# Score steps and weight requests kept away from the joined attention-times-V blocks

## The chip, the cores and the metric

The kernel runs on one core of one Trainium2 chip. The core has a matrix engine (TensorE, PE in the profile, with its weight loads as PEld), three elementwise engines (VectorE = DVE, ScalarE = ACT, GpSimd = POOL), a queue engine (SyncE = SP) that issues most transfers, and 16 DMA engines. The engines run side by side, each through its own instructions in order, and wait for each other on semaphores. The metric is device time in microseconds (us), the median of several executions of one program.

## The reference, cut to what matters

```python
x = A_x                                   # 1 x 2048 x 576, bf16
xn = _layernorm(x)
# A: attention, 32 heads of 18, causal, window of 256 positions
qkv = (xn @ wqkv) ...
scores = einsum("bhqd,bhkd->bhqk", q, k) * (Dh ** -0.5)
mask = (i - j >= 0) & (i - j < 256)
p = softmax(where(mask, scores, -1e9))
a = (einsum("bhqk,bhkd->bhqd", p, v)) @ wo
# B: gated MLP, F = 4608
b = (silu(xn @ w1) * (xn @ w3)) @ w2
return x + a + b
```

Both branches read the same normalised input, and their results are added.

## The kernel before

The 2048 rows are cut into four chunks of 512. Every chunk runs through three stages. First come the projections for q, k and v. Then follows the long stage in which the gate and up products of the MLP are mixed with the attention. The last stage ("phase 2", `p2_list`, L809) multiplies with w2 and wo and adds the input.

The mixed stage is a loop over 36 **units** (`for u in range(NF)`). A unit makes 128 columns of the hidden layer. It is nine **pairs** of matmuls (`unit_pairs`, L738); the two matmuls of a pair use the two halves of the array and run at the same time. After its nine pairs a unit has one tanh on ACT (`unit_tanh`, L747) and two products on DVE (`unit_h`, L753 and L756). A unit takes one of three pairs of PSUM banks (`JOBS`, handed out in turn by `job()`).

Between the pairs the planner puts the attention:

- A **score step** (`score_step`) is four or six short matmuls of q and k into the PSUM banks 6 and 7 (`scores`, L612), one exp on ACT (`exps`, L621) and the masks on POOL (`masks`, L648). A chunk from 1 on has 40 of them. There is only one pair of score banks, so a step's matmuls wait until the exp of the step before has read them. When a step is due is a running sum in units of one pair (`clock`, `nxt`, `soon`).
- An **attention-times-V block** (`pv`, L669) multiplies the probabilities of the steps with V. In chunks 1 to 3 the first block is a *joined* one for two head groups at once (`BLOCKS[c][0] == (0, 1)`). It stands at a fixed place in the middle of a unit (`AT`), takes two pairs of banks, and is drained by four transposes on DVE (`pv_out`, L685), then reciprocals, scalings on POOL (L694) and turns on DVE (L701). A single block `(2,)` follows later at the end of a unit, and a last one in phase 2.
- The finished outputs are sent to `oT` by small transfers on SP's queue (`o_pack`, L726): four for head group 0 and eight smaller ones, two at a time after four successive units, then four for head group 1.

The **weights** w1 and w3 are used in blocks of four units; nine blocks make a chunk. They lie in three buffers `w13`. A buffer is filled by six requests of 192 KB on SP's queue (`load_part`, L322). Six requests become owed (`owed += 6`) after units 3, 7, 11 and so on up to 27, when a block has been used up, for the block after the next two. One owed request is recorded behind pair 3 and one behind pair 8 of a unit (`owe_part`), and waits for that pair's matmul. The first matmul of a block waits for all six requests of its buffer, since all are writers of the key `("w13", sl)`:

```python
r=[("w13", sl)] + (["xnS"] if 4 <= n < 8 else xk(c)), ...
```

Every engine works through its operations in the order in which the Python code records them. SP's queue too is in order: a request behind the small transfers waits until those have been issued.

Phase 2 begins with two short groups of matmuls with wo. The first writes the free pair of banks from `JOBS`, the second the score banks 6 and 7 (`ACC[:] = [[*JOBS[job_ctr % 3], *SC], ...]`), which the exp of the chunk's last score step (number 39, counted from 0) must have read.

Of the kernel before, what the change touches and what calls it, by code (L numbers as in the profile page):

```python
# [164 lines left out]
def bass_parallel_sum__sliding_block__glu_gated_swiglu__prompt_kernel(  # L165
# [21 lines left out]
    NF = F // 128  # L187
# [10 lines left out]
    with ExitStack() as es:  # L198
# [74 lines left out]
        def job():  # L273
            nonlocal job_ctr
            i = job_ctr % 3
            job_ctr += 1
            return JOBS[i]
# [56 lines left out]
        def owe_part(op):  # L334
            nonlocal owed
            if owed:
                owed -= 1
                load_part((op,))
# [338 lines left out]
        def borrow(slots):  # L677

            for i, n in enumerate(slots):
                uqs[2 + i:3 + i] = [pt[:, n, :, :].rearrange("p q r -> p (q r)").bitcast(dt.float32)]  # L680
                uq_keys[2 + i:3 + i] = [[("pt", n)]]

        def pv_out(b, i):
            to = uqs[i]
            add("dve", lambda e: e.transpose(to, PS[:, b, :]), r=[("ps", b)], w=uq_keys[i])  # L685

        def o_recip(i):
            u3 = uqs[i].rearrange("p (n d) -> p n d", d=32)
            add("dve", lambda e: e.reciprocal(rden[i][:], u3[:, :, Dh]), r=uq_keys[i], w=[("rden", i)])

        def o_scale(i):
            u3 = uqs[i].rearrange("p (n d) -> p n d", d=32)
            o3 = oq[:, :].rearrange("p (n d) -> p n d", d=32)[:, :, 0:Dh]
            add("pool", lambda e: e.tensor_tensor(  # L694
                o3, u3[:, :, 0:Dh], rden[i][:].unsqueeze(2).to_broadcast([128, CH // 32, Dh]), ALU.mult),
                r=uq_keys[i] + [("rden", i), "oq0"], w=["oq"])
# [307 lines left out]
        BLOCKS = [((0,), (1,), (2,))] + [((0, 1), (2,))] * 3  # L1004
        PV_AFTER = (20, 18, 18, 18)
        START = (60, 46, 46, 46)
        AT = ((NF, 0), (18, 3), (18, 5), (18, 7))
        main, rest = span_main, span_last
        late_spans = {0: [(main, 2, 5, 0, 1, "act")], 1: [(main, 2, 5, 1, 2, "act"), (main, 2, 5, 2, 5, "sp")],
                      **{u: [(rest, 2, 5, u - 2, u - 1, "act")] for u in (2, 3, 4)},  # L1010
# [3 lines left out]
        for c in range(NC):  # L1014
            NS = len(steps_of(c))
            att = [(g, s) for g in range(G) for s in range(NS)]
# [13 lines left out]
            nxt = soon = start  # L1030
            clock = 0.0
            done = 0
            pv_ready = {}
            free = [("pt", n) for n in range(NPT)]
            free += [("sh", n) for n in range(4)]
            early = [("h", n) for n in range(4 if c == 0 else 0, NHP)]
            side = {}
            jobs = {}
            next_pv = 0
            turned = {}  # L1040

            def later(u, what):
                side.setdefault(u, []).append(what)
# [25 lines left out]
            def pv_block(u, mid=False):  # L1069
                nonlocal next_pv, clock, free, job_ctr, nxt, soon  # L1070
                block = BLOCKS[c][next_pv]
                assert u > turned.get(c, -1) + 1, (c, u, turned)
                next_pv += 1
                pairs = [job() for _ in block]
                for j, banks in zip(block, pairs):
                    pv(c, j, banks)
                clock += PV_COST * len(block)
                if len(block) == 2:
                    nxt, soon = max(nxt, clock + 14), max(soon, clock + 14)
                groups = range(2 * block[0], 2 * block[-1] + 2)  # L1080
                was = [pt_of[(c, g, s)] for g in groups for s in range(NS)]
                assert all(NF - 2 * NHP + 2 * n > u for kind, n in was if kind == "h"), (c, u)
                was = [sl for sl in was if sl[0] != "h"]
                lent = [n for kind, n in was if kind == "pt"][-2:] if len(block) == 2 else []
                free += [sl for sl in was if sl not in [("pt", n) for n in lent]] + [("pt", n) for n in lent]

                def drain(pairs=pairs, lent=lent):
                    borrow(lent)
                    for i in range(2 * len(pairs)):
                        pv_out(pairs[i // 2][i % 2], i)  # L1090
                    for i in range(2 * len(pairs)):
                        o_recip(i)
                    o_scale(0)

                drain() if mid else later(u, drain)
                job_ctr += mid
                k = 0
                for i, g in enumerate(groups):
                    for half in range(2):
                        k += 1 if (i, half) not in ((0, 1), (2, 1)) else 0  # L1100
                        later(u + k, lambda g=g, half=half: o_turn(g, half))
                    if i + 1 < len(groups):
                        later(u + k, lambda i=i: o_scale(i + 1))
                turned[c] = u + k
                for i, j in enumerate(block):
                    later(u + (4 + 3 * i if c else 5), lambda j=j: o_pack(j, "sp"))
                    for n in range(4, 12, 2 if c else 1) if j == 0 else ():
                        later(u + n // 2 + 3 if c else u + n + 1,
                              lambda n=n: o_pack(0, "sp", n, n + 2) if c else o_pack(0, "act", n, n + 1))
# [19 lines left out]
            for u in range(NF):  # L1129
                at_u = u  # L1130
                if c == 0 and u == 0:
                    owed += 6
                if u in loads:
                    for i in loads[u]:
                        xslot[(c + 1) * TB + i] = load_x((c + 1) * TB + i)
                b0 = jobs[u] = job()
                for n in range(9):
                    into = nxt - (clock + 9 - n)
                    if done < len(att) and (done < len(early) or free) and (clock >= nxt or (n == 8 and into < 3 and clock >= soon)):
                        spaced_step()  # L1140
                    if next_pv == 0 and AT[c] == (u, n):
                        pv_block(u, True)
                    op = unit_pairs(c, u, n, n + 1, b0[0])
                    clock += 1
                    if n in (3, 8):
                        owe_part(op)
                unit_tanh(u, b0[0])
                if u % 4 == 3 and u < NF - 8 and (c or u != 15):
                    owed += 6
                if next_pv in pv_ready and clock >= pv_ready[next_pv] and (next_pv or not AT[c][1]):  # L1150
                    pv_block(u)
                unit_h(u, b0[0])
                for what in side.pop(u, []):
                    what()
                if u in stat:
                    t = (c + 1) * TB + stat[u]
                    for part in range(3):
                        ln_stats(t, xslot[t], part)
                if u in xt:
                    xn_send((c + 1) * TB + xt[u])  # L1160
                if u in apply:
                    t = (c + 1) * TB + apply[u]
                    ln_apply(t, xslot[t])
                for span, a, b, n0, n1, eng in late_spans.get(u, []) if c == 0 else []:
                    span(a, b, only=slice(n0, n1), **({"q_eng": eng} if span is main else {"eng": eng}))
                if c == 0 and u == 8:
                    add("dve", lambda e: e.memset(oT[:, 4, :].bitcast(dt.float32), 0.0), w=["oTz"])
                if c == 0 and u == 13:
                    for t in range(4):
                        r0 = 4 * Dh + 252 * (t // 2)  # L1170
                        rows = A_wo[r0:r0 + 252, :].rearrange("(s p d) f -> p s d f", p=2, d=Dh)[t % 2, :, :, :]
                        add("sp", lambda e, t=t, rows=rows: e.dma_start(wo[0:126, t, :], rows),
                            dma="wo", **{"j" if t else "w": ["wo"]})
                if c == 0 and u == 18:
                    rows = A_wo[0:4 * Dh, :].rearrange("(n d) f -> n d f", d=Dh)
                    add("sp", lambda e: e.dma_start(wo[126:128, 0:4, :], rows[:, 0:2, :].rearrange("n d f -> d n f")),
                        j=["wo"], dma="wo")
                    for p in range(2):
                        add("sp", lambda e, p=p: e.dma_start(wo[64 * p:64 * p + 64, 4, :], rows[:, 2:Dh, :]),
                            j=["wo"], dma="wo")  # L1180
                if c == 0 and u in (20, 22, 24, 26):
                    load_w2(0, (u - 20) // 2, "act" if u < 24 else "sp")
                if u == 31:
                    xs = [load_x(c * TB + tt) for tt in range(TB)]
# [9 lines left out]
            n = -3  # L1194
# [62 lines left out]
```

## Time and profile before

| | |
|---|---|
| median of 3 runs | 558.32 us (557.24 to 558.74) |
| profiled execution, its own time | 558.11 us |
| its span, first to last instruction | 556.4 us |
| granted TensorE clock | 1.00 |
| PE busy | 551.5 us, 99% of the span |
| DVE, ACT, POOL busy | 313.0, 260.3, 160.6 us |
| HBM read | 71.29 MB |

The profile's own time is longer than its span by 1.7 us, which lie outside the instructions. In the views, a row of the timeline or of the chain of waits has the start in us from the span's start, then the duration, the engine, the line of the kernel, and the number of instructions merged into it; a square bracket tells how long the engine sat idle before it, and what ended that. PE's matmuls overlap, so that a row's duration is longer than the time until the next one starts.

### The profile page before, as it was taken

The numbers are of one execution on the slowest core, as the hardware profiler recorded it, in microseconds if no ns is written. First come the engines' busy times: TensorE is split into PE (matmuls) and PEld (weight loads), VectorE is DVE, ScalarE is ACT, GpSimd is POOL, SyncE is SP. The second block draws the span as 40 slices with busy tenths as digits, with TensorE's granted clock in tenths as the row PEclk, the third lists the DMA queues.
The fourth block names the chain that finished last, engine by engine and source line by source line (L and its number), as shares of the span: only waits on it lengthen the run. The fifth ranks groups of instructions, "written<-read, shape, count | busy, mean of one in ns | idle before, by whom it ended". The sixth has DMA issues, their size and how long they took to land.

```text
span 556.4 us, 18249 instructions
## 1 busy us (share of the span) xinstructions
PE 551.5 (99%) x8022; PEld 365.3 (66%) x8022; DVE 313.0 (56%) x587; ACT 260.3 (47%) x365; POOL 160.6 (29%) x380
## 2 busy tenths in 40 slices
PE   8999999999999999999999999999999999999998
PEld 4555445677688855577776665557777667555776
DVE  7466798520468887741056887773105566868211
ACT  7456776100387757600047775760005677676000
POOL 4323454300035435430003533452000333343000
PEclk9999999999999999999999999999999999999999
DMA  9998898567567953656846895365684685332660
GB/s 252 214 202 179 191 207 204 143 179 185 140 142 170 163 144 102 165 138 186 196 106 138 171 187 132 89 165 155 156 202 91 138 176 153 105 103 67 162 164 23
DMA packets 128038, 86.00 MB, mean 155 GB/s; under 512 B 35702, under 2 KB 125646, under 8 KB 127958
## 3 DMA queue, kind: packets, MB, share of 16 engines
q1 hardware_dynamic: 89138, 62.80, 50.1%
q10 hardware_dynamic: 38820, 22.02, 15.6%
q8 instruction: 63, 1.03, 0.8%
q14 instruction: 17, 0.14, 0.1%
HBM read 71.29 MB, written 2.36 MB: 132 GB/s over the span
## 4 chain that ended last, share of the span: by engine, by line
PE 98%; DMA 1%; ACT 0%; DVE 0%; issue 0%
PE ps L738 51%; PE ps L809 29%; PE ps L492 10%; PE ps L612 6%; PE ps L669 3%; DMA xp<-in_A_x_dram 1%; DVE stats L388 0%; ACT hT L382 0%; PE ps L421 0%; ACT sd L361 0%; DVE ofin L831 0%; ACT xnT L434 0%; DVE mv L391 0%
## 5 line engine op out<-in xcount | busy, mean ns | idle before, releaser
L738 PE MATMUL ps<-xnT,w 64*128 64x512 bf16 x1400 | 187.9, 376 | 0.0
L738 PE MATMUL ps<-xnS,w 64*128 64x512 bf16 x1120 | 157.4, 376 | 0.0
L809 PE MATMUL ps<-w,hT 64*128 64x288 bf16 x2292 | 143.9, 282 | 0.0
L753 DVE SCALAR_TENSOR_TENSOR gs<-th,ps 128x512 bf16<-128x512 bf16 x144 | 98.1, 681 | 76.6 <-ACT th L747 75.8
L809 PEld LDWEIGHTS ps<-w,hT 64*128 64x128 bf16 x2292 | 111.8, 94 | 29.6 <-issue 0.2
L738 PEld LDWEIGHTS ps<-xnT,w 64*128 64x128 bf16 x1400 | 83.3, 94 | 51.9 <-issue 0.7
L621 ACT ACTIVATE pt<-ps 128x1024 bf16<-128x1024 f32 (+1 forms) x92 | 93.2, 1013 | 42.0 <-PE ps L612 41.7
L747 ACT ACTIVATE th<-ps 128x512 bf16<-128x512 f32 x144 | 85.6, 595 | 34.3 <-PE ps L738 33.7
L756 DVE SCALAR_TENSOR_TENSOR hT<-gs,ps 128x512 bf16<-128x512 bf16 x144 | 98.9, 687 | 4.9
L738 PEld LDWEIGHTS ps<-xnS,w 64*128 64x128 bf16 x1120 | 65.6, 94 | 41.9
L648 POOL TENSOR_TENSOR pt<-pt,mk 128x128 int32<-128x128 int32 (+1 forms) x164 | 67.4, 435 | 51.8 <-ACT pt L621 51.7
L505 ACT ACTIVATE stage<-ps 128x512 bf16<-128x512 f32 x16 | 9.6, 598 | 142.8 <-PE ps L492 140.5
L648 POOL TENSOR_TENSOR hT<-hT,mk 128x128 int32<-128x128 int32 (+1 forms) x52 | 20.8, 421 | 165.0 <-ACT hT L621 165.0
L840 DVE TENSOR_TENSOR ofin<-ps,xp 128x288 bf16<-128x288 f32 x31 | 12.2, 451 | 89.0 <-PE ps L809 89.0
L612 PE MATMUL ps<-qv,kv 64*128 64x320 bf16 (+4 forms) x528 | 55.8, 260 | 0.0
L612 PEld LDWEIGHTS ps<-qv,kv 64*128 64x128 bf16 x528 | 31.4, 94 | 21.6 <-ACT pt L621 0.5
L621 ACT ACTIVATE stage<-ps 128x1024 bf16<-128x1024 f32 (+1 forms) x32 | 32.4, 1011 | 15.6 <-PE ps L612 14.1
L492 PE MATMUL ps<-xnT,wp 64*128 64x512 bf16 (+1 forms) x360 | 39.1, 355 | 0.0
L621 ACT ACTIVATE hT<-ps 128x1024 bf16<-128x1024 f32 (+1 forms) x28 | 28.5, 1016 | 10.0 <-PE ps L612 9.9
L648 POOL TENSOR_TENSOR stage<-stage,mk 128x128 int32<-128x128 int32 (+1 forms) x56 | 22.0, 413 | 26.8 <-ACT stage L621 26.7
L492 PEld LDWEIGHTS ps<-xnT,wp 64*128 64x128 bf16 x360 | 20.6, 94 | 12.5 <-ACT va L541 0.4
L701 DVE STREAM_TRANSPOSE od<-oq 128x256 bf16<-128x256 bf16 x64 | 25.8, 427 | 3.1 <-POOL oq L694 3.1
(76 smaller groups left out, 344.2 us busy)
## 6 DMA issues: line engine op xcount, KB each, us to landing
w<-in_B_w_dram SPq DMA_DIRECT2D x210, 192.0 KB, 4.1
w<-in_B_w_dram ACTq DMA_DIRECT2D x70, 288.0 KB, 3.5
xp<-in_A_x_dram SPq DMA_DIRECT2D x29, 144.0 KB, 3.4
out_dram<-ofin SPq DMA_DIRECT2D x31, 72.0 KB, 3.1
xnS<-xnT SPq DMA_DIRECT2D x8, 256.0 KB, 5.2
oT<-od SPq DMA_DIRECT2D x56, 36.0 KB
pt<-in_A_wqkv_dram SPq DMA_DIRECT2D x4, 288.0 KB, 5.4
hT<-in_B_w_dram SPq DMA_DIRECT2D x6, 192.0 KB, 6.2
```

Of the source, the lines that this page charges most:

```text
L492: op = add("pe", lambda e, out_=out_, st=st, mv=mv, n=n, r0=r0, first=first: e.matmul(out_, st, mv, start=first, stop=(part == 1 and n == ...
L612: add("pe", lambda e, r0=r0, out_=out_, kb=kb, q0=q0, nb=nb: e.matmul(out_, kb4[r0:r0 + 64, g, kb + NV - NB, :] if kb < 0 else kv[r0:r0 + ...
L621: add("act", lambda e: e.activation(pt_slot(sl)[:, 0:w, :], PS[:, SC[0]:SC[1] + 1, 0:w].rearrange("p r q -> p q r"), ACT.Exp, scale=scale) ...
L648: add("pool", lambda e, vb=vb, mm=mm: e.tensor_tensor(vb, vb, mm, ALU.mult), r=(key if n == 0 else []) + ["mk"], **{"w" if n == 0 else "j" ...
L669: add("pe", lambda e, p=p, q=q, pr=pr, sl=sl, g=g, pos=pos, q0=q0, nb=nb, col=col, first=first, n=n: e.matmul(PS[32 * q:32 * q + VW, banks ...
L701: add("dve", lambda e: e.transpose(od[i][:, g % 2, c0:c0 + CH // 2], oq[:, c0:c0 + CH // 2]), r=["oq", "oq0"], **{"j" if half or g % 2 els ...
L738: op = add("pe", lambda e, n=n, r0=r0, r=r, k=k, src=src: e.matmul(PS[:, b0 + r, :], wt[r0:r0 + 64, k, fl * 128:(fl + 1) * 128], src, star ...
L747: add("act", lambda e: e.activation(th[i][:], PS[:, bg, :], ACT.Tanh, scale=0.5), r=[("ps", bg)], w=[("th", i)])
L753: add("dve", lambda e: e.scalar_tensor_tensor(out=gs[i][:], in0=th[i][:], scalar=1.0, in1=PS[:, bg, :], op0=ALU.add, op1=ALU.mult), r=[("t ...
L756: add("dve", lambda e: e.scalar_tensor_tensor(out=hT[:, u, :], in0=gs[i][:], scalar=0.5, in1=PS[:, bu, :], op0=ALU.mult, op1=ALU.mult), r= ...
L809: op = add("pe", lambda e: e.matmul(PS[:, bank, 0:w], stat, move, start=new, stop=False, skip_group_check=True, **tile), r=keys, after=hel ...
L840: add("dve", lambda e: e.tensor_tensor(ofin[:, o, :], PS[:, bank, 0:HD], xp[xs[n]][:, d0:d0 + HD], ALU.add), r=[("ps", bank), ("xp", xs[n] ...
```

## The change

```diff
-        AT = ((NF, 0), (18, 3), (18, 5), (18, 7))
+        HOLD = 15
+        AT = ((NF, 0), (18, 8), (19, 1), (19, 3))
...
                 if len(block) == 2:
-                    nxt, soon = max(nxt, clock + 14), max(soon, clock + 14)
+                    nxt, soon = max(nxt, clock + 17), max(soon, clock + 17)
...
                     into = nxt - (clock + 9 - n)
-                    if done < len(att) and (done < len(early) or free) and (clock >= nxt or (n == 8 and into < 3 and clock >= soon)):
+                    ahead = 9 * (AT[c][0] - u) + AT[c][1] - n
+                    still = next_pv == 0 and 0 <= ahead < HOLD
+                    if not still and done < len(att) and (done < len(early) or free) and (clock >= nxt or (n == 8 and into < 3 and clock >= soon)):
                         spaced_step()
...
-                    if n in (3, 8):
+                    if n in (3, 8) and not (c and 16 <= u < 20):
                         owe_part(op)
```

Four things change in chunks 1 to 3; chunk 0 stays as it was.

1. The joined block comes five pairs later: chunk 1 from unit 18 pair 3 to unit 18 pair 8, chunk 2 from (18, 5) to (19, 1), chunk 3 from (18, 7) to (19, 3).
2. In the 15 pairs ahead of it no score step is put, and behind it the next one comes 17 instead of 14 counts later.
3. No weight request is recorded in units 16 to 19.
4. What follows from these by the planner: the steps that were held come later and closer, and the requests move.

The requests of the mixed stage, by the unit whose pairs 3 and 8 they stand behind (the same in chunks 1 to 3, save that chunk 3 has no last row):

| weight block | first used in unit | before, units | after, units |
|---|---|---|---|
| 6 | 24 | 16 to 18 | 20 to 22 |
| 7 | 28 | 20 to 22 | 23 to 25 |
| 8 | 32 | 24 to 26 | 26 to 28 |
| 0 of the next chunk | its first | 28 to 30 | 29 to 31 |

The small transfers to `oT` after the joined block stand in SP's queue after units 22 to 26 before, and in chunk 1 still do. In chunks 2 and 3 they stand one unit later now. In order, of chunk 1 after the change: four behind unit 22, two behind 23, two behind 24, six behind 25 (two of head group 0, four of group 1), two behind 26. In chunks 2 and 3: four behind unit 23, two behind 24, two behind 25, six behind 26, two behind 27.

The score steps in the changed program:

| | chunk 1 | chunk 2 | chunk 3 |
|---|---|---|---|
| none between | (16, 3) and (20, 7) | (17, 3) and (21, 0) | (16, 8) and (21, 2) |
| spacing behind it, pairs | 7 | 7 | 7 |
| steps between pair 8 of unit 22 and unit 24 | 2 | 1 | 1 |
| from the first pair of unit 24 to that of unit 28 | 5 | 6 | 5 |
| from the first pair of unit 28 to that of unit 32 | 5 | 5 | 6 |
| single block ahead of unit (before: 30 in all) | 32 | 31 | 32 |
| step 39 ahead of pair (before: unit 34 pair 7) | (35, 8) | (34, 8) | (35, 8) |

Before, the steps behind the joined block are mostly 8 pairs apart and at the end 9, and the joined block of chunk 1 has a step right ahead of it. The number of matmuls, exps, masks and transfers is the same in both programs.

## The prediction

> **What bounds the kernel now.** I read the page first: busy times, then the chain of work that ended last, then the transfers.
>
> ```profile
> span 556.4 us, 18249 instructions
> PE 551.5 (99%) x8022; PEld 365.3 (66%) x8022; DVE 313.0 (56%) x587; ACT 260.3 (47%) x365; POOL 160.6 (29%) x380
> PE 98%; DMA 1%; ACT 0%; DVE 0%; issue 0%
> ```
>
> PE sets the end nearly everywhere, so any wait that PE gets is paid in full, and a gain can come only out of time in which PE stands. The sums over the three mixed stages (chunks 1, 2, 3) show how much of that there is: stretch, length, then busy time of each engine, clock, DMA share, GB/s.
>
> ```profile
> 155.42:237.83 82.41, 82.41 (x1125) 57.08 (x1122) 63.15 (x116) 58.71 (x76) 36.27 (x87) 1.00 0.68 149
> 292.57:375.58 83.01, 82.45 (x1124) 50.04 (x1122) 62.88 (x116) 58.81 (x76) 36.23 (x87) 1.00 0.71 148
> 430.32:512.65 82.33, 82.33 (x1125) 49.49 (x1122) 56.89 (x96) 57.94 (x76) 32.34 (x76) 1.00 0.51 123
> ```
>
> PE is busy without a break in chunks 1 and 3, and stands for 83.01 - 82.45 = 0.56 us in chunk 2. The chain of waits has it (start, length, what), the timeline says where it falls, and the sums around it what the DMA engines did:
>
> ```profile
> 333.00 2.50 PE ps L669 x157
> 338.84 0.56 issue
> ```
>
> ```profile
> 339.40 0.19 PE L612 MATMUL ps<-qv,kb 64*128 64x64 bf16 x1 [0.56 <-issue]
> 333.00:336.00 3.00, 3.00 (x198) 2.50 (x200) 2.39 (x5) 0.63 (x1) 0.75 (x2) 1.00 1.14 213
> 338.40:339.60 1.20, 0.64 (x12) 0.32 (x8) 0.73 (x2) 0.60 (x1) 0.00 (x0) 1.00 0.30 99
> ```
>
> The wait is in a score step 3.4 us behind the joined block (333.00 to 335.49); nothing that the profile shows released it ("issue"). In the block PE works through 198 matmuls and 200 weight loads in 3 us while the DMA engines are full (share 1.14); I take it for instructions that came late. It is the only thing this change could win.
>
> **The price list.** From the chain of waits (start, length, what):
>
> ```profile
> 361.21 1.30 PE ps L669 x93
> 364.56 0.22 PE ps L612 x4
> 364.78 1.94 PE ps L738 x18
> ```
>
> A unit of nine pairs is 1.94 us (a pair 0.216), a score step 0.22, a single block 1.30. Now one unit of chunk 1 in the timeline of PE, and SP's queue from the same place on:
>
> ```profile
> 207.72 1.24 PE L738 MATMUL ps<-xnT,w 64*128 64x512 bf16 x10
> 208.80 0.38 PE L612 MATMUL ps<-qv,kv 64*128 64x320 bf16 x4
> 209.02 1.03 PE L738 MATMUL ps<-xnS,w 64*128 64x512 bf16 x8
> 209.88 1.03 PE L738 MATMUL ps<-xnT,w 64*128 64x512 bf16 x8
> ```
>
> ```profile
> 208.14 0.60 SPq L322 DMA_DIRECT2D w<-in_B_w_dram  x1
> 208.78 4.75 SPq L726 DMA_DIRECT2D oT<-od  x6
> 213.57 1.32 SPq L322 DMA_DIRECT2D w<-in_B_w_dram  x2
> 214.93 1.30 SPq L726 DMA_DIRECT2D oT<-od  x2
> 216.28 1.32 SPq L322 DMA_DIRECT2D w<-in_B_w_dram  x2
> 217.64 4.45 SPq L726 DMA_DIRECT2D oT<-od  x6
> 222.13 1.42 SPq L322 DMA_DIRECT2D w<-in_B_w_dram  x2
> ```
>
> The ten matmuls at 207.72 are pair 8 of unit 22 and the first four pairs of unit 23. The request behind pair 8 goes out at 208.14, 0.42 us after that pair starts. Unit 24 starts one pair after 209.88, at 210.10. On SP's queue six small transfers hold up what follows by 4.79 us (208.78 to 213.57) or 4.49 (217.64 to 222.13), two of them by 1.35, two requests by 1.36, one by 0.64 (208.14 to 208.78). Time from request to landing, min/median/max over the 23 requests from 185 to 226 us, and of the one at 208.14 alone:
>
> ```profile
> DMA to landing us min/median/max: 3.1/3.6/4.1
> w<-in_B_w_dram SPq DMA_DIRECT2D x1, 192.0 KB, 3.5
> ```
>
> I take 3.5 us, the row with the very surroundings of the critical request, and keep 3.1 and 4.1 as ends.
>
> **Part 1, block 6 in unit 24.** Before, its last request stands behind unit 18, five units ahead of its use. Now it stands behind pair 8 of unit 22. Count from the start of that pair: request at 0.42, landed at 0.42 + 3.5 = 3.92. PE reaches unit 24 after one pair, unit 23 and its score steps: 0.22 + 1.94 + 0.22 = 2.38 in chunks 2 and 3 (the trace itself has 210.10 - 207.72 = 2.38 for that), 2.60 with the two steps of chunk 1. PE waits 1.32, 1.54 and 1.54 us, **4.4 us** together. With landings of 3.1 or 4.1 it is 3.2 or 6.2. Even the quickest landing misses the unit, so this term cannot vanish. Nothing can cover it: the wait is in PE's own queue ahead of all later pairs and steps.
>
> [...]
>
> **Part 2, blocks 7 and 8 behind the small transfers.** Their requests now come close behind block 6's, in a queue that before already lagged (requests behind unit 24 went out at 213.57, when SP had worked off the six small transfers). I run the queue on from the same zero.
>
> Chunk 1: SP free at 1.06; four small transfers (4/6 of 4.79, an estimate: 3.19) to 4.25; two requests to 5.61; two small to 6.96; two requests to 8.32; two small to 9.67; the last two requests of block 7 go out at 9.67 and 10.35, landed 13.85. PE has started unit 24 at 3.92 and needs 4 x 1.94 and five steps, 3.92 + 7.77 + 1.10 = 12.79: it waits **1.06** for unit 28. Then six small to 15.52, two requests to 16.88, two small to 18.23, two requests to 19.59, the last at 20.27, landed 23.77. PE: 13.85 + 7.77 + 1.10 + 1.30 for the single block = 24.02: no wait.
>
> Chunks 2 and 3: the first two requests of block 7 go out ahead of the small ones, the second when pair 8 of unit 23 has started (2.58), SP free at 3.24; four small to 6.43; then in turns of 1.36 and 1.35 to 9.14; last request 9.82, landed 13.32. PE reaches unit 28 at 13.01 (six steps) and 12.79 (five): waits **0.31 and 0.53**. On: 10.50, two small 11.85, two requests 13.21, six small 17.70, two requests 19.06, two small 20.41, last request 21.09, landed 24.59. PE reaches unit 32 at 13.32 + 7.77 + 1.30 + 1.10 = 23.49 and with six steps 23.71: waits **1.10 and 0.88**.
>
> Part 2 is 3.9 us. Bounds: 0 if SP works off its queue 1.1 us quicker per chunk, and some 3 us more if a request's issue drags in each chunk, as it does at times (1522 ns at most instead of a median of 614, in chunk 2):
>
> ```profile
> L322 SPq DMA_DIRECT2D w<-in_B_w_dram x18: 595/614/1522, 340.3 to 367.3; - x18
> ```
>
> **Part 3, the start of phase 2.** Step 39 moves from unit 34 to one pair ahead of the end in chunks 1 and 3. Its exp must have left banks 6 and 7 before the second short group of phase 2. In chunk 1 before (step at 235.07, exp to 236.53, phase 2 at 237.67) there is room:
>
> ```profile
> 235.07 0.27 PE L612 MATMUL ps<-qv,kb 64*128 64x256 bf16 x2
> 235.50 1.03 ACT L621 ACTIVATE pt<-ps 128x1024 bf16<-128x1024 f32 x1 [0.43 <-PE ps L612]
> 237.67 0.41 PE L809 MATMUL ps<-wo,oT 64*128 64x288 bf16 x4
> ```
>
> The exp ends 1.46 us after the step begins. Now PE gets there after the step (0.22), a pair (0.22) and the first group (half of the 0.24 from 237.67 to the next at 237.91, 0.12): 0.56. It waits 0.9 us in each of the two chunks, **1.8 us**; ACT could add to it, and only another order of PE's could take it away.
>
> ```profile
> 237.91 1.27 PE L809 MATMUL ps<-w,hT 64*128 64x288 bf16 x18
> ```
>
> **Part 4, at little or nothing.** The number of steps and blocks stays, so PE's own work does. Steps 7 pairs apart are 7 x 0.216 + 0.22 = 1.73 us apart, and the exp is gone after 1.46: 0.27 to spare. A step ahead of a unit's first pair (five in all) finds ACT in the tanh of the unit before and may lose some 0.1 us; most of it falls into the waits above, which shrink by as much. In chunk 1 the joined block ends one pair before unit 19, which writes the block's first banks. DVE needs 713 + 668 ns for them from the block's middle on:
>
> ```profile
> L685 DVE STREAM_TRANSPOSE uq<-ps 128x512 f32<-128x512 f32 x13 | 9.3, 713 | 26.6 <-PE ps L669 26.4
> L685 DVE STREAM_TRANSPOSE ofin<-ps 128x512 f32<-128x512 f32 x13 | 8.7, 668 | 0.0
> ```
>
> 1.38 against 1.30 + 0.22 = 1.52 us on PE: hidden, 0 to 0.3 us if DVE starts late. The gain is the 0.56 us of chunk 2, between 0 (the wait moves to where the requests now bunch) and 0.56.
>
> **The sum.** 4.4 + 3.9 + 1.8 - 0.6 = 9.5 us on the profile's own 558.11 gives 567.6. That execution is 0.2 us under the median of 558.32, which I leave aside: forecast **567.5 us**, 1.6% slower. Low end: landings of 3.1 and a quick SP queue, 3.2 + 0 + 0 - 0.6, 560.7, unlikely all together; high end 6.2 + 3.9 + 3 + 1.8 - 0, 573.
>
> **The rivals.**
>
> - *Only the first deadline is missed.* SP catches up or the queue's lag costs less than I count, so part 2 is gone: 4.4 + 1.8 - 0.6, 563.7 us. For it: the waits of part 2 are small differences of long sums. Against: each wait of PE moves later requests back too.
> - *The other side: instructions come in time and the weights too.* The mechanism is the change's own: without requests and steps around the joined block, PE's instructions arrive, and the 0.56 us of chunk 2 goes. It decides if a request lands within 2.38 - 0.42 = 1.96 us. Then the time is 557.5 to 558, no difference that can be told. Against it stands the minimum of 3.1. A gain over 0.3% would need 1.7 us of PE standing still, and the stages have 0.56.
> - *PE's clock drops in the waits.* If each of my ten waits (two, three and three in parts 1 and 2, two in part 3) were followed by some 3 us at half speed, it would cost 1.5 us apiece, 15 more: 582. Against: the clock stays 1.00 across the 0.56 us wait in the sums above, though no wait of 1.5 us is in these stages. [...]
> - *The queue drags.* Slow issues in each chunk make parts 1 and 2 some 5 us larger: 572 to 573.
>
> **How the numbers follow.** Forecast 0.74, first deadline only 0.12, the other side 0.05, clock 0.02, dragging queue 0.07. The range 562 to 572 us holds the forecast with its bounds and the first rival, and leaves about 0.15 outside. A difference below 0.3% (1.7 us) cannot be told from none. Slower by more than that: all cases but the second rival, 0.94; within: 0.04; faster: 0.02, for what I may have missed.
>
> **What would show it.** Right: PE idle ahead of L738, ended by a DMA of w, about 1.3 to 1.5 us once in each of chunks 1 to 3 (unit 24), and shorter ones four and eight units on; an idle of 0.9 us ahead of L809 ended by ACT's exp at the start of phase 2 in chunks 1 and 3; PE's busy time in the mixed stages unchanged; no "issue" wait near 339. Wrong: no such waits, landings under 2 us, or waits of PE on ACT or DVE in the middle of the units.

## The result, and the profile after

| | before | after |
|---|---|---|
| median of 6 runs | 557.78 us (557.21 to 558.74) | 575.32 us (573.90 to 579.01) |
| ratio, 95% interval | | 1.032 [1.029, 1.035] |
| profiled execution, its own time | 558.11 us | 576.36 us |
| its span | 556.4 us | 574.6 us |

The change makes the kernel 17.5 us slower; the forecast was 9.5. The direction and the kinds of waits are as predicted, the size is not. The profiled execution lies 1.0 us above the median, and its span grew by 18.2 us; the accounts below are of that execution.

The page of the changed kernel: the span, the busy times, the chain of work that ended last, and the group of matmuls that opens a unit (behind the bar its busy time, the mean in ns, the idle time ahead of it and what ended that).

```profile
span 574.6 us, 18249 instructions
PE 555.7 (97%) x8022; PEld 374.2 (65%) x8022; DVE 312.5 (54%) x587; ACT 260.4 (45%) x365; POOL 160.7 (28%) x380
PE 92%; DMA 4%; issue 2%; ACT 1%; DVE 1%; SPq 0%
L738 PE MATMUL ps<-xnT,w 64*128 64x512 bf16 x1400 | 192.8, 377 | 12.7 <-DMA w<-in_B_w_dram 7.7
```

Before, the same group had no idle time ahead of it:

```profile
L738 PE MATMUL ps<-xnT,w 64*128 64x512 bf16 x1400 | 187.9, 376 | 0.0
```

The number of instructions is the same. PE was the chain to 98%; now it is 92%, 4% of it is DMA, and the group that opens the units has 12.7 us of idle time ahead of it. The sums over the three mixed stages say where: first before, cut at the same instructions as after (first matmul of the first unit to first matmul of phase 2), then after.

```profile
155.14:237.67 82.53, 82.53 (x1127) 57.20 (x1122) 63.25 (x116) 58.99 (x76) 36.11 (x86) 1.00 0.68 149
292.36:375.42 83.06, 82.50 (x1125) 50.05 (x1121) 62.90 (x116) 59.02 (x76) 36.07 (x86) 1.00 0.71 148
430.12:512.49 82.37, 82.37 (x1124) 49.49 (x1121) 56.90 (x96) 58.14 (x76) 32.34 (x76) 1.00 0.51 123
```

```profile
154.99:242.58 87.59, 83.00 (x1125) 62.69 (x1121) 63.28 (x117) 58.02 (x75) 34.73 (x83) 1.00 0.65 139
298.25:387.91 89.66, 84.78 (x1125) 51.54 (x1122) 62.88 (x116) 59.19 (x76) 35.88 (x86) 0.98 0.64 136
442.62:529.76 87.14, 83.11 (x1124) 50.46 (x1121) 57.37 (x97) 57.19 (x75) 31.65 (x75) 1.00 0.46 116
```

The stages grew by 5.06, 6.60 and 4.77 us, 16.4 together. PE stands for 87.59 - 83.00 = 4.59, 4.88 and 4.03 us. Its busy time grew as well, by 0.47, 2.28 and 0.74 us, though it does the same work. Some 0.2 us of that, an estimate, go with each wait: a matmul's row (377 ns in the mean) is longer than the 216 ns until the next pair starts, and at a wait this overlap is lost. What is left over in chunk 2, about 1.5 us, goes with a clock of 0.98. The rest of the 18.2 us is at the start of phase 2 in chunks 1 and 3, about 1 us each. The view of waits (engine, tile, line, releaser: us in total, times, longest) gives PE's two largest:

```profile
PE ps L738 <- DMA w<-in_B_w_dram: 7.7, 5, 2.4
PE ps L738 <- issue: 5.0, 4, 2.1
```

The timeline of PE places them, and the four smaller ones in the joined blocks (L669) and at the start of phase 2 (L809):

```profile
210.52 1.04 PE L738 MATMUL ps<-xnT,w 64*128 64x512 bf16 x8 [0.92 <-issue]
221.98 1.04 PE L738 MATMUL ps<-xnT,w 64*128 64x512 bf16 x8 [2.38 <-DMA w<-in_B_w_dram]
233.72 1.04 PE L738 MATMUL ps<-xnT,w 64*128 64x512 bf16 x8 [1.29 <-DMA w<-in_B_w_dram]
243.66 0.30 PE L809 MATMUL ps<-wo,oT 64*128 64x288 bf16 x2 [0.78 <-ACT pt L621]
341.66 0.56 PE L669 MATMUL ps<-pt,va 64*20 64x320 bf16 x24 [0.57 <-DVE hT L756]
354.53 0.39 PE L738 MATMUL ps<-xnT,w 64*128 64x512 bf16 x2 [0.97 <-issue]
365.06 1.04 PE L738 MATMUL ps<-xnT,w 64*128 64x512 bf16 x8 [1.27 <-DMA w<-in_B_w_dram]
377.58 0.90 PE L738 MATMUL ps<-xnT,w 64*128 64x512 bf16 x4 [2.06 <-issue]
485.91 1.00 PE L669 MATMUL ps<-pt,va 64*20 64x320 bf16 x60 [0.27 <-DVE hT L756]
498.41 0.82 PE L738 MATMUL ps<-xnT,w 64*128 64x512 bf16 x6 [1.03 <-issue]
508.51 0.61 PE L738 MATMUL ps<-xnT,w 64*128 64x512 bf16 x4 [1.06 <-DMA w<-in_B_w_dram]
520.90 1.04 PE L738 MATMUL ps<-xnT,w 64*128 64x512 bf16 x8 [1.68 <-DMA w<-in_B_w_dram]
530.85 0.29 PE L809 MATMUL ps<-wo,oT 64*128 64x288 bf16 x2 [0.78 <-ACT pt L621]
```

In each chunk the three waits ahead of L738 are those for units 24, 28 and 32. Four of the nine are put down to "issue", but they are waits for weights too, as the transfers show. For the first of them, here is the last request of block 6 in chunk 1, and its time to landing:

```profile
207.24 0.59 SPq L322 DMA_DIRECT2D w<-in_B_w_dram  x1
```

```profile
w<-in_B_w_dram SPq DMA_DIRECT2D x1, 192.0 KB, 3.2
```

207.24 + 3.2 = 210.44, and PE goes on at 210.52. The clock after the longest wait of chunk 2 (stretch, length, busy times, then the clock as the third number from the end):

```profile
376.00:377.50 1.50, 0.00 (x0) 0.00 (x0) 0.80 (x2) 0.64 (x2) 1.02 (x3) 1.00 1.08 228
377.50:381.30 3.80, 3.72 (x22) 1.86 (x24) 1.26 (x3) 1.02 (x1) 0.67 (x1) 0.55 1.14 227
```

For about 3.4 us (0.45 of 3.8 us missing, at half speed) PE ran at half clock; from 378.50 to 380.50 the clock is 0.50. Of the six executions three have a mean clock of 1.000 (573.90 to 575.30 us), so that stretch is not in every one.

SP's queue in chunk 1, from behind the request above to block 8:

```profile
207.88 3.40 SPq L726 DMA_DIRECT2D oT<-od  x4
211.33 1.40 SPq L322 DMA_DIRECT2D w<-in_B_w_dram  x2
212.77 1.34 SPq L726 DMA_DIRECT2D oT<-od  x2
214.16 2.18 SPq L322 DMA_DIRECT2D w<-in_B_w_dram  x2
216.38 1.30 SPq L726 DMA_DIRECT2D oT<-od  x2
217.72 1.33 SPq L322 DMA_DIRECT2D w<-in_B_w_dram  x2
219.09 4.44 SPq L726 DMA_DIRECT2D oT<-od  x6
...
226.42 7.42 SPq L322 DMA_DIRECT2D w<-in_B_w_dram  x10
```

Block 7's requests stand in turn with the small transfers, as predicted. The last two go out from 217.72 on. The prediction's chain had them at 9.67; with its zero at 206.82, so that its request at 0.42 is the one at 207.24, that is 206.82 + 9.67 = 216.49.

### The profile page after: what moved, and what is told of

It reads as the page before. It is cut to its first block, busy times and chain, and to the rows that moved or that the text cites. A ratio compares the mean times of both kernels' runs of the same rounds, so it can differ in the third digit from the quotient of the medians.

```text
span 574.6 us, 18249 instructions
## 1 busy us (share of the span) xinstructions
PE 555.7 (97%) x8022; PEld 374.2 (65%) x8022; DVE 312.5 (54%) x587; ACT 260.4 (45%) x365; POOL 160.7 (28%) x380
## 4 chain that ended last, share of the span: by engine, by line
PE 92%; DMA 4%; issue 2%; ACT 1%; DVE 1%; SPq 0%
PE ps L738 47%; PE ps L809 28%; PE ps L492 9%; PE ps L612 5%; DMA w<-in_B_w_dram 4%; PE ps L669 2%; DMA xp<-in_A_x_dram 0%; ACT pt L621 0%; DVE hT L756 0%; DVE gs L753 0%; ACT th L747 0%; DVE stats L388 0%; ACT hT L382 0%; PE ps L421 0%; ACT sd L361 0%
## 5 line engine op out<-in xcount | busy, mean ns | idle before, releaser
L738 PE MATMUL ps<-xnT,w 64*128 64x512 bf16 x1400 | 192.8, 377 | 12.7 <-DMA w<-in_B_w_dram 7.7
L738 PE MATMUL ps<-xnS,w 64*128 64x512 bf16 x1120 | 159.8, 378 | 0.0
L809 PE MATMUL ps<-w,hT 64*128 64x288 bf16 x2292 | 143.9, 282 | 0.0
L809 PEld LDWEIGHTS ps<-w,hT 64*128 64x128 bf16 x2292 | 112.9, 94 | 28.6 <-issue 0.4
L738 PEld LDWEIGHTS ps<-xnT,w 64*128 64x128 bf16 x1400 | 87.2, 94 | 63.6 <-DMA w<-in_B_w_dram 11.9
L738 PEld LDWEIGHTS ps<-xnS,w 64*128 64x128 bf16 x1120 | 69.5, 94 | 37.8 <-issue 0.5
L492 PE MATMUL ps<-xnT,wp 64*128 64x512 bf16 (+1 forms) x360 | 39.0, 355 | 0.0
L492 PEld LDWEIGHTS ps<-xnT,wp 64*128 64x128 bf16 x360 | 20.5, 94 | 12.6 <-ACT va L541 0.4
L694 POOL TENSOR_TENSOR oq<-uq,rden 128x288 bf16<-128x288 f32 x13 | 8.8, 674 | 67.3 <-DVE rden L689 67.3
```

What stands on the lines that cost most here:

```text
L492: op = add("pe", lambda e, out_=out_, st=st, mv=mv, n=n, r0=r0, first=first: e.matmul(out_, st, mv, start=first, stop=(part == 1 and n == ...
L738: op = add("pe", lambda e, n=n, r0=r0, r=r, k=k, src=src: e.matmul(PS[:, b0 + r, :], wt[r0:r0 + 64, k, fl * 128:(fl + 1) * 128], src, star ...
L809: op = add("pe", lambda e: e.matmul(PS[:, bank, 0:w], stat, move, start=new, stop=False, skip_group_check=True, **tile), r=keys, after=hel ...
```

## The experiments

Times are medians, each ratio is against the kernel before on the same chip.

**The request rule alone.** Once it is taken out of the changed kernel, once put alone into the kernel before.

```diff
-                    if n in (3, 8) and not (c and 16 <= u < 20):
+                    if n in (3, 8):
```

> The changed kernel with the old rule for requests (behind pairs 3 and 8 of every unit); joined block, hold and spacing as changed. Theory (late requests cost nearly all, some 13.5 us of PE's waits in units 24, 28 and 32 and 1.7 us of half clock behind one of them): 560 to 561 us, no wait of PE for w in the mixed stages; what is left is about 1 us at the start of phase 2 in chunks 1 and 3 and about 1 us in the joined blocks of chunks 2 and 3. Rival (the denser score steps or the later block cost as much themselves): over 565 us.

Measured: 561.14 us, ratio 1.006 [1.005, 1.008]. No wait for weights is left in any chunk; the waits at phase 2 and in the joined block stay. The mixed stage of chunk 2 in the sums:

```profile
293.88:377.78 83.90, 83.06 (x1125) 49.59 (x1122) 62.76 (x116) 58.98 (x76) 35.70 (x86) 1.00 0.71 146
```

It is back within 0.8 us of before; those of chunks 1 and 3 (82.94 and 82.88 us) within 0.4 and 0.5. So the request rule costs 575.3 - 561.1 = 14.2 us.

```diff
-                    if n in (3, 8):
+                    if n in (3, 8) and not (c and 16 <= u < 20):
```

> The kernel before with the new rule for requests alone (none in units 16 to 19). Theory: 570 to 573 us, with waits of PE for w at units 24, 28 and 32 of chunks 1 to 3 of the changed kernel's size, none at the start of phase 2 or in the joined blocks. Rival (the requests are late only together with the moved block and steps): under 563 us.

Measured: 571.86 us, ratio 1.025 [1.024, 1.027], 14.0 us: the two ways of taking the rule agree in the total, though not in its parts. In detail the expectation missed. Units 24 and 28 wait in all three chunks, but unit 32 only in chunk 3, for 0.7 us (0.52 us of idle time and the lost overlap); what makes the time up is two stretches at half clock, behind the waits of unit 28 in chunks 1 and 2. In chunk 2 the clock is 0.79 over 8 us (364.00 to 372.00), 1.7 us missing. The stretch in chunk 1, first in the timeline of PE, then in the sums:

```profile
222.14 1.53 PE L738 MATMUL ps<-xnT,w 64*128 64x512 bf16 x8 [2.00 <-DMA w<-in_B_w_dram]
```

```profile
223.00:226.40 3.40, 3.40 (x24) 1.70 (x22) 0.00 (x0) 1.23 (x2) 0.31 (x1) 0.56 0.37 100
```

**The small transfers out of the requests' way.** In the changed kernel the transfers of the joined block go out three units later in chunks 1 to 3.

```diff
-                    later(u + (4 + 3 * i if c else 5), lambda j=j: o_pack(j, "sp"))
+                    later(u + (4 + 3 * i + 3 * (len(block) == 2) if c else 5), lambda j=j: o_pack(j, "sp"))
...
-                        later(u + n // 2 + 3 if c else u + n + 1,
+                        later(u + n // 2 + 3 + 3 * (len(block) == 2) if c else u + n + 1,
```

> The changed kernel with the small transfers to oT of the joined block three units later, so that the requests of weight block 7 stand ahead of them in SP's queue. Theory (units 28 and 32 are late because of SP's queue behind the small transfers): the waits at unit 24 stay at 1.1 us or so each, those at 28 and 32 (some 10 us of the sum) shrink to under 3 us, the half clock goes: 564 to 567 us. Rival (it is the time from request to landing, or the chain of one late block on the next, whatever stands between in the queue): 572 us or more.

Measured: 570.01 us, ratio 1.020 [1.018, 1.023], between the ranges of theory and rival. The four executions scatter (567.62 to 572.61 us), and the profiled one is the longest: it also has a wait of 2.5 us for the DMA of `wv` (L492), which is loaded once at the start, far ahead of the mixed stages that the edit touches, and its mean clock is 0.994. Chunks 1 and 3 did as the theory said: only unit 24 waits, and their stages shrank to 83.78 and 84.19 us. Chunk 2 has a cost of the experiment's own. The single block comes a unit earlier there, its turns on DVE wait until the late transfers have read `od` (the longest such wait of the run is 5.2 us), and the products of the last units queue behind them on DVE:

```profile
383.53 1.69 PE L738 MATMUL ps<-xnT,w 64*128 64x512 bf16 x8 [3.20 <-DVE hT L756]
```

Behind it the clock is 0.60 over 4.00 us (383.00 to 387.00), 1.6 us missing. So chunk 2 was run again with two units instead of three.

```diff
-                    later(u + (4 + 3 * i if c else 5), lambda j=j: o_pack(j, "sp"))
+                    later(u + (4 + 3 * i + (2 if c == 2 else 3) * (len(block) == 2) if c else 5), lambda j=j: o_pack(j, "sp"))
...
-                        later(u + n // 2 + 3 if c else u + n + 1,
+                        later(u + n // 2 + 3 + (2 if c == 2 else 3) * (len(block) == 2) if c else u + n + 1,
```

> As the run with the small transfers three units later, but in chunk 2 only two units later, so that they are over before the single block's turns on DVE need their buffer. Theory (SP's queue behind the small transfers made the waits at units 28 and 32): waits for w at unit 24 alone, about 1.2 us in each of chunks 1 to 3, no half clock in the mixed stages; 564 to 566 us, which is the run with the old rule for requests plus 3.6 us. Rival (lateness passes from block to block even with a free queue): 568 us or more in undisturbed runs, with waits for w at unit 28 or 32.

Measured: 566.34 us, ratio 1.015 [1.013, 1.017]. Units 28 and 32 wait in no chunk, and the clock is 1.00. The sums of chunks 1 and 3, and what is left of the side effect in chunk 2 (DVE's turn, then PE):

```profile
155.00:238.72 83.72, 82.70 (x1127) 61.71 (x1121) 63.17 (x117) 58.04 (x76) 34.62 (x83) 1.00 0.65 140
434.94:519.00 84.06, 82.80 (x1124) 50.46 (x1121) 57.41 (x97) 57.19 (x76) 31.56 (x75) 1.00 0.48 120
```

```profile
376.16 0.77 DVE L701 STREAM_TRANSPOSE od<-oq 128x256 bf16<-128x256 bf16 x2 [3.20 <-DMA oT<-od]
...
378.29 1.04 PE L738 MATMUL ps<-xnT,w 64*128 64x512 bf16 x8 [1.19 <-DVE hT L756]
```

The small transfers standing in front of blocks 7 and 8 are worth at least 575.3 - 566.3 = 9.0 us of the 14, the half clock included; the side effect, a wait of 1.2 us, hides some of it.

**Catching up.** The changed kernel keeps its pause in units 16 to 19, and records four requests a unit instead of two in units 20 to 22.

```diff
-                    if n in (3, 8) and not (c and 16 <= u < 20):
+                    if (n in (3, 8) or c and 20 <= u < 23 and n in (1, 5)) and not (c and 16 <= u < 20):
```

> The changed kernel with four requests instead of two in each of units 20 to 22 (behind pairs 1, 3, 5 and 8), so that block 6 is requested by (21, 3) and block 7 by (22, 8), as before; still none in units 16 to 19. Theory: no wait for w, the time of the run with the old rule for requests within 1 us, 560 to 561 us. Rival (requests bunched in three units land so late, or take instructions and the small transfers along, that PE waits elsewhere): over 563 us.

Measured: 561.12 us, ratio 1.006 [1.005, 1.008], the same as without the pause. Only unit 24 of chunks 2 and 3 still waits a little:

```profile
349.43 0.39 PE L738 MATMUL ps<-xnT,w 64*128 64x512 bf16 x2 [0.57 <-issue]
```

So the pause itself is not the cost; it is that the requests stay late behind it.

**A shorter pause.** The changed kernel with three units without requests instead of four.

```diff
-                    if n in (3, 8) and not (c and 16 <= u < 20):
+                    if n in (3, 8) and not (c and 16 <= u < 19):
```

> The changed kernel with no requests in units 16 to 18 instead of 16 to 19: every request of the blocks 6 to 8 one unit (2.2 us) earlier. Theory (each wait is the landing of a block's last request against PE's arrival, and SP's queue behind the small transfers is what remains late): the waits at unit 24, 1.1 us or so, vanish whole, unit 28 waits 0 to 0.6 us, unit 32 still 1 to 2 us in each chunk; 565 to 567 us with the 3.3 us of the start of phase 2 and the joined blocks. Rival (the deadline of unit 24 starts the lateness of all later blocks): 561 to 562 us, as with the old rule.

Measured: 565.35 us, ratio 1.013 [1.012, 1.015]. Unit 24 waits nowhere. What is left is unit 28 in chunk 1 and unit 32 in chunks 1, 2 and 3:

```profile
219.43 0.82 PE L738 MATMUL ps<-xnT,w 64*128 64x512 bf16 x6 [0.62 <-issue]
231.61 0.82 PE L738 MATMUL ps<-xnT,w 64*128 64x512 bf16 x6 [1.71 <-issue]
371.79 1.04 PE L738 MATMUL ps<-xnT,w 64*128 64x512 bf16 x8 [0.91 <-issue]
509.99 0.82 PE L738 MATMUL ps<-xnT,w 64*128 64x512 bf16 x6 [0.68 <-issue]
```

Requests one unit (1.94 us and its score steps) earlier save 10.0 us: five of the nine waits for weights end, and three are shorter. That of unit 32 in chunk 1 is longer, 1.71 against 1.29 us, since PE comes there 2.5 us earlier (231.61 - 1.71 = 229.90 against 233.72 - 1.29 = 232.43) and the weights only 2.1 us.

**The block moved alone.** The kernel before with the new places only.

```diff
-        AT = ((NF, 0), (18, 3), (18, 5), (18, 7))
+        AT = ((NF, 0), (18, 8), (19, 1), (19, 3))
```

> The kernel before with the new places of the joined block alone (AT): no hold, spacing 14, old rule for requests. Theory (the joined block of chunks 2 and 3 comes so early in unit 19 that its second pair of banks, that of unit 18, is not yet read by DVE): PE waits in the joined block for DVE's hT, about 0.9 us in chunk 2 and 0.4 in chunk 3, nothing in chunk 1, step 39 stays in unit 34; 558.5 to 560 us. Rival (the wait in the block comes from the held and bunched steps): 558 us or less, no wait in the block.

Measured: 560.85 us, ratio 1.006 [1.004, 1.007], more than expected. In chunk 2 PE, in the middle of the joined block, waits for DVE's product of unit 18, and behind the block stands a wait that no releaser explains, longer than the one before the change:

```profile
336.09 1.00 PE L669 MATMUL ps<-pt,va 64*20 64x320 bf16 x60 [0.61 <-DVE hT L756]
340.92 0.37 PE L738 MATMUL ps<-xnT,w 64*128 64x512 bf16 x1 [0.77 <-issue]
```

```profile
335.35 0.69 DVE L756 SCALAR_TENSOR_TENSOR hT<-gs,ps 128x512 bf16<-128x512 bf16 x1
```

The product ends at 335.35 + 0.69 = 336.04, and PE goes on at 336.09. The block takes two pairs of banks. From (19, 1) on, unit 19 holds one of the three; the block's first half gets that of unit 17, and the second that of unit 18, which ended only one or three pairs earlier and whose products DVE has not finished. Chunk 3 has the same wait, 0.57 us of idle time; chunk 1, whose block still stands in unit 18, has none.

**The steps held alone.** The changed kernel with the old places of the block and the old request rule.

```diff
-        AT = ((NF, 0), (18, 8), (19, 1), (19, 3))
+        AT = ((NF, 0), (18, 3), (18, 5), (18, 7))
...
-                    if n in (3, 8) and not (c and 16 <= u < 20):
+                    if n in (3, 8):
```

> The changed kernel with the old places of the joined block and the old rule for requests: what is left is the hold of 15 pairs and the spacing of 17. Here step 39 comes in unit 35 in chunk 3 alone. Theory: 0.95 us at the start of phase 2 of chunk 3, none in chunks 1 and 2, no wait in the joined block; 558 to 559 us. Rival (denser steps cost of themselves, by the one pair of score banks): 560 us or more, with waits of PE on exp in the mixed stages.

Measured: 558.89 us, ratio 1.002 [1.001, 1.004]. The one wait of note is the start of phase 2 in chunk 3, and the 0.9 us over before are about what it costs:

```profile
513.10 0.30 PE L809 MATMUL ps<-wo,oT 64*128 64x288 bf16 x2 [0.78 <-ACT pt L621]
```

**A pause that fits.** The kernel before, with no requests in units 17 and 18 only.

```diff
-                    if n in (3, 8):
+                    if n in (3, 8) and not (c and u in (17, 18)):
```

> The kernel before with no requests in units 17 and 18 alone, so that block 6 is requested by unit 20 and block 7 by unit 23, still four units ahead of their use. Theory (PE's wait of 0.56 us for instructions behind the joined block comes from the requests that bunch there): no such wait and no wait for w; 557.2 us, up to 0.6 us under the kernel before, which a measurement can hardly tell. Rival (that wait is there in some executions whatever the requests do): the same time, with a wait that the profile calls issue near the joined block of some chunk.

Measured: 557.40 us, ratio 0.999 [0.998, 1.001]: not told apart from before. In the profiled execution the wait of chunk 2 is gone, and PE is busy throughout the stage:

```profile
292.25:374.60 82.35, 82.35 (x1124) 49.50 (x1121) 62.87 (x116) 58.85 (x76) 36.07 (x86) 1.00 0.68 149
```

That is the 0.56 us which the change could win at most; the interval is too wide to show it in the time.

## Why the prediction was wrong in size

The terms of the sum against the profiled execution. A measured wait is the idle time of its row plus 0.2 us of lost overlap.

| term | predicted | measured |
|---|---|---|
| unit 24, chunks 1, 2, 3 | 1.32, 1.54, 1.54 = 4.4 | 1.1, 1.2, 1.2 = 3.5 |
| unit 28 | 1.06, 0.31, 0.53 = 1.9 | 2.6, 1.5, 1.3 = 5.4 |
| unit 32 | 0, 1.10, 0.88 = 2.0 | 1.5, 2.3, 1.9 = 5.7 |
| start of phase 2 | 1.8 | 2.0 |
| joined block | 0 to 0.3 | 0.8 + 0.5 = 1.3 |
| half clock, chunk 2 | 0 (rival) | 1.5 |
| wait of chunk 2 | -0.6 | -0.6 |
| sum | 9.5 | 18.8, against 18.2 in the span |

**Part 1 was right**, 0.9 us too high: the last requests of block 6 landed in 3.2, 3.0 and 3.1 us in chunks 1 to 3, and 3.5 were assumed. Taking out the request rule takes out these waits.

**Part 2 is the step that failed**, by size: 3.9 us predicted, 11.1 measured. The mechanism holds, since sending the small transfers later removes all six waits, and so does catching up with the requests. The size was a difference of long sums, each with an error to the same side. In chunk 1 the last two requests of block 7 go out 217.72 - 216.49 = 1.2 us later than the chain had them: four small transfers took 3.45 instead of 3.19, and two requests 2.22 (214.16 to 216.38) instead of 1.36, a slow issue of the kind that the prediction kept for its rival. PE came about 0.2 us earlier, since unit 24 had waited less. 1.06 + 1.2 + 0.2 = 2.5 us, against the measured 2.6. At unit 32 of chunk 1 the landing added its part. Ten requests go out back to back from 226.42 on, and the last one of block 8 is in a pair that took 5.0 us instead of 3.5:

```profile
w<-in_B_w_dram SPq DMA_DIRECT2D x2, 192.0 KB, 5.0
```

In chunks 2 and 3 PE came 0.3 to 0.4 us earlier to unit 28, and the rest was mostly the queue again. In chunk 2 a pair of small transfers took 2.25 us, not 1.35; in chunk 3 two requests took 0.99 and 1.15 us.

```profile
370.88 2.25 SPq L726 DMA_DIRECT2D oT<-od  x2
```

The upper bound of "some 3 us more" counted one slow issue per chunk only. PE's earlier arrival and the longer landing were no part of it. At all six deadlines the two chains lay within 1.1 us of a tie, so that errors of either came through in full: the six waits are 0.8 to 1.5 us longer than forecast.

**Part 3 was right**: 0.78 us of idle time and the lost overlap at phase 2 in chunks 1 and 3, ended by ACT's exp.

**Part 4 missed a term.** It looked at the banks of the unit behind the joined block, and not at those that the block itself takes over. Moving the block alone shows that wait, in chunks 2 and 3.

**The rivals.** The dragging queue, given 0.07, is nearest to what came: slow issues in each chunk. But part 1 did not grow, and it took PE's earlier arrival and the longer landing as well to pass its 572 to 573 us. The clock rival, given 0.02, was right in kind for one of the thirteen waits. Its 3 us at half speed were an assumption that no row of before shows; in the changed kernel the stretch behind the wait of 2.06 us lasted about 3.4 us. The predicted loss per drop was 1.5 us, and that is what this one cost.

The parts taken alone add up: the request rule 14.0, the block 560.85 - 558.01 = 2.8, the steps 0.9, together 17.7 us against 17.5 for the whole change. That they meet so closely is in part luck. The block alone has an unexplained wait of 0.77 us which the changed kernel does not have, and the steps alone wait at phase 2 once, the changed kernel twice. Block and steps together, without the request rule, measured 561.14 - 557.82 = 3.3 us, not 3.7.

## What to carry to other kernels

Before holding requests back in a queue that runs in order, count how far ahead of its use the last request of each block stands, and what else stands in the same queue behind the pause: the delay is paid again at each later deadline, until the requests catch up. Where a chain of queue times and a chain of matmuls come out within 1 us of each other, give the wait a range instead of the difference; here six such waits came out 0.8 to 1.5 us too short. Moving work between units also changes whose banks it takes over; look at who still reads those.

## What the runs showed of the hardware

- PE's clock was at half for about 3.4 us directly behind an idle time of 2.06 us (changed kernel, chunk 2; 0.55 over 3.80 us), and at 0.56 over 3.40 us behind one of 2.00 us (request rule alone, chunk 1), but the changed kernel's row for chunk 1 has 2.38 us, and the clock stays at 1.00:

```profile
222.00:225.40 3.40, 3.40 (x36) 1.97 (x38) 0.53 (x2) 1.69 (x3) 0.74 (x2) 1.00 0.25 50
```

  With the request rule alone, an equal wait of 2.38 us (chunk 2) was followed by a clock of 0.79 over 8 us. So the length of the wait alone does not decide; what else does stays open.
- One issue on SP's queue took 0.61 us for a weight request and 0.70 us for a small transfer, in the median of either kernel, but single ones took far longer: before, 1.52 us for a request (chunk 2) and 1.24 us for a small transfer (chunk 1); after the change 1.48 us for a request of chunk 1 and 1.56 us for a small transfer of chunk 2.
- The waits "issue" of 0.56 us (before), 0.77 us (block moved) and 0.27 us (changed kernel with the old request rule) come about 3 us behind the end of the joined block of chunk 2, where requests go out around it. They are absent in the profiles with a pause in the requests ahead of the block, and in that with the steps held. That instructions came late there was only argued, and each profile is one execution.
